# 103 products of zeros in several array forms, issued behind TensorE's warm-up

## The chip, the cores and the metric

The kernel runs on one core of one Trainium2 chip. The metric is the device time of one execution in microseconds (us); the times given are those of undisturbed executions.

## The reference

A block over 2048 rows of width 512. The input is normalized once, and the sum of three terms is returned: the input, an attention over 32 heads of width 16, and a gated MLP whose gate mixes the rows with a 2048 x 2048 matrix.

```
xn = layernorm(x)                                   # x: 1 x 2048 x 512
# attention: 32 heads, head width 16
q, k, v = split(xn @ wqkv)                          # wqkv: 512 x 1536
A = (softmax(q @ k.T * 16**-0.5) @ v) @ wo          # per head; wo: 512 x 512
# gated MLP: inner width 2 x 896
z = gelu(xn @ w_in)                                 # w_in: 512 x 1792
g = w_sp @ layernorm(z[:, 896:]) + b_sp             # w_sp: 2048 x 2048
B = (z[:, :896] * g) @ w_out                        # w_out: 896 x 512
return x + A + B                                    # all in float32
```

## The kernel before

All work of the program is written out ahead of time; each engine runs its own list in order, and a planner in the kernel (`rollout`, `length`) chose TensorE's order for the long phase.

**Front phase.** `load_x` loads the rows in four groups of four tiles of 128 rows. `norm_x` computes mean and variance on VectorE (L391, L392), the factors on ScalarE and VectorE (L394 to L396) and normalizes on ScalarE (L400). `turn_x` transposes the tiles on TensorE (L408) into banks of PSUM; `split` copies each bank as a high part on ScalarE (L78) and subtracts it for a low part on VectorE (L218), which gives `xnT`. Products of the front phase take three multiplications of such parts each (`mm3`, L221 to L223). `v_first` and `v_tile` make the values `v` (L546, L549), `qk_group` the first queries and keys. The weights are split by GpSimd (L1165, L322, L327, L328), partly by VectorE (L322).

**Long phase.** It runs over 16 pairs of heads, four chunks of 512 queries and 16 tiles of keys. TensorE's array is used in several forms there. A *half* is a product of up to 64 rows by 128 columns on the upper or lower half of the rows: the scores (`score`, `st`, L1291), the products from which the maxima are taken (`mx`, L922), and the dense products of the MLP and of the projections (L233). Two halves stand side by side. A *column quad* is four products of 128 rows by 32 columns, side by side on the columns, in plain float32: the product of the weights with the values (`pv`, `o`, L1249). At the end come products of 32 rows (L1109) and quads of another width (L1071).

**Ahead of it all** stands the warm-up: `WARM = 15` products of zeros over the whole array, from the tile `idle` (a piece of the `big` ring, `RING = 25` buffers), which VectorE clears at L1146. They write a bank of PSUM that nobody reads. TensorE's next entry behind them is the first transposition of `turn_x`, L408. The banks `r0` to `r4` are handed out by `rsum`; the first four go to `turn_x`.

A tile of the type `F32R` is multiplied in one pass; the same bytes seen as `F32` (`bitcast`) leave two records per product in the trace.

Of the kernel before, what the change touches and what calls it, by code (L numbers as in the profile page):

```python
# [11 lines left out]
F32 = mybir.dt.float32  # L12
# [7 lines left out]
P = 128  # L20
# [35 lines left out]
def fused_block(ctx, tc, x, wqkv, wo, w_in, w_spT, b_sp, w_out, out):  # L56
    nc = tc.nc
# [5 lines left out]
    ps = ctx.enter_context(tc.tile_pool(name="ps", bufs=1, space=PSUM))  # L63
# [52 lines left out]
    def raw(t):  # L116
        return t.bitcast(F32) if t.dtype == F32R else t
# [3 lines left out]
    def move(dst, src):  # L121
        dma[0] = max(dma[0], clock()) + 0.1 + 4e-6 * math.prod(dst.shape) / FLOW
        nc.sync.dma_start(raw(dst), raw(src))
# [71 lines left out]
    def piece(nm):  # L195
        return big.tile([P, 2, 512], F32R, tag="big", name=nm, bufs=RING)
# [167 lines left out]
    def load_x(g):  # L364
        xt = [at.tile([P, 2, D], F32, tag="pf", name=f"x{g}_{i}", bufs=PF) for i in (0, 2)]
        for i in range(len(xt)):
            k = 2
            t = 4 * g + k * i
            for j in range(k):
                xs[g, k * i + j] = xt[i][:, j, :]  # L370
            if g == 0:
                for j in range(k):
                    move(xt[i][:, j, :], x[(t + j) * P:(t + j + 1) * P, :])
                    yield
            else:
                move(xt[i], x[t * P:(t + k) * P, :].rearrange("(a p) d -> p a d", p=P))
# [758 lines left out]
    def init_rows(a):  # L1135

        for j in range(2):
            row = 64 * j + KS
            for r in range(2):
                nc.gpsimd.dma_start(raw(kst[a])[row + r:row + r + 1, :], cscr[0:1, :])  # L1140

    engines = {mybir.EngineType.PE, mybir.EngineType.Activation, mybir.EngineType.DVE, mybir.EngineType.Pool, mybir.EngineType.SP}
    with tc.manual_schedule(engines=engines):
        nc.scalar.activation(mhalf, epst, AF.Sqrt)
        idle = piece("idle")
# [2 lines left out]
        rest = dpsum("idle", "o")  # L1148
        for _ in range(WARM):
            nc.tensor.matmul(rest, idle[:, 0, 0:P], idle[:, 0, :], start=True, stop=True)  # L1150
        first = load_x(0)
        next(first)
        next(first)
# [488 lines left out]
```

## Time and profile before

| | |
|---|---|
| median of 2 runs | 1789.35 us (1789.29 to 1789.4) |
| span of the profiled execution | 1786.8 us |
| what the median has beside that span | 2.55 us |
| TensorE busy (matmul) | 1775.9 us, 99%, 14419 records |
| TensorE busy (weight load) | 1136.6 us, 64% |
| VectorE busy | 1448.4 us, 81% |
| ScalarE busy | 1267.0 us, 71% |
| GpSimd busy | 782.2 us, 44% |
| mean granted TensorE clock | 0.999 |

The profile is of one execution on the chip. PE is TensorE's multiplication, PEld its weight load, DVE VectorE, ACT ScalarE, POOL GpSimd, SP SyncE. In the timeline a row gives start and length in us, engine, line of the kernel, operation, output and inputs, the form (rows*columns), the shape and a count; in brackets stands the idle time before it and what ended it. A matmul's end is modelled, and records of successive products overlap; therefore distances are best taken from start to start. In a table of stages each engine has its busy time and its number of instructions; PEclk is the clock that TensorE was granted.

### The profile page before, as it was taken

The page shows a single profiled execution, that of the slowest core. Times are in us where ns is not written, and L with a number is a line of the kernel's source. Part 1 is how long each engine was busy: PE and PEld are TensorE (multiplying, and loading weights), DVE is VectorE, ACT ScalarE, POOL GpSimd, SP SyncE. Part 2 cuts the span into 40 slices and gives each one's busy share as a digit, 9 for nine tenths or more (in the row PEclk, how much of TensorE's full clock was granted, in tenths as well). Part 3 has the DMA queues.
Part 4 walks back from the last instruction along what each step waited for, and adds up shares of the span by engine and source line. Part 5 has one row for each costly group of instructions (what it writes and reads, how often), then busy time and mean ns, then how long its engine had stood idle before and what let it go on. Part 6 is the DMA issues. An engine that isn't in the chain of part 4 may idle for free.

```text
span 1786.8 us, 37962 instructions
## 1 busy us (share of the span) xinstructions
PE 1775.9 (99%) x14419; PEld 1136.6 (64%) x14419; DVE 1448.4 (81%) x2604; ACT 1267.0 (71%) x2351; POOL 782.2 (44%) x815
## 2 busy tenths in 40 slices
PE   9999999999999999999999999999999999999998
PEld 7876666666666666656566566666666666666664
DVE  5288888988888888888888888888877888888872
ACT  5338788887777777777777777777776777677765
POOL 4257677777312542257334573224765261004220
PEclk9999999999999999999999999999999999999999
DMA  8552443534645744355446564345666454454534
GB/s 287 200 168 77 133 128 102 171 88 125 199 151 171 234 133 111 115 167 181 135 142 178 171 193 117 105 126 165 197 181 176 145 171 134 147 170 150 155 113 135
DMA packets 218254, 274.63 MB, mean 154 GB/s; under 512 B 35752, under 2 KB 119352, under 8 KB 216632
## 3 DMA queue, kind: packets, MB, share of 16 engines
q1 hardware_dynamic: 215336, 263.47, 48.8%
q0 software_dynamic: 2592, 8.46, 1.2%
q8 instruction: 114, 1.87, 0.5%
q14 instruction: 68, 0.56, 0.1%
q10 hardware_dynamic: 144, 0.26, 0.0%
HBM read 178.55 MB, written 93.58 MB: 152 GB/s over the span
## 4 chain that ended last, share of the span: by engine, by line
PE 97%; DVE 1%; DMA 1%; ACT 1%; POOL 0%; SPq 0%; issue 0%; DVEq 0%; ACTq 0%; POOLq 0%
PE o L1249 26%; PE st L1291 18%; PE sp L233 17%; PE mx L922 13%; PE z2p L233 5%; PE mo L233 4%; PE z1p L233 4%; PE ao L233 2%; PE qk L233 2%; PE duo L233 2%; PE v L221 0%; PE v L222 0%; PE v L223 0%; PE xT L408 0%; PE qk L223 0%; PE qk L221 0%
## 5 line engine op out<-in xcount | busy, mean ns | idle before, releaser
L923 DVE TENSOR_REDUCE mm<-mx 128x1 f32<-128x512 f32 x2048 | 1290.6, 684 | 249.5 <-PE mx L922 216.3
L1294 ACT ACTIVATE pf<-st 128x512 f32<-128x512 f32 x2048 | 1102.6, 601 | 362.3 <-PE mx L922 216.8
L1291 PE MATMUL st<-qst,kst 50*128 50x512 f32 x2048 | 764.4, 410 | 0.9 <-ACT pf L1294 0.7
L922 PE MATMUL mx<-kst,qst 48*128 48x512 f32 x2048 | 752.5, 412 | 0.1
L1291 PEld LDWEIGHTS st<-qst,kst 50*128 50x128 f32 x2048 | 361.1, 185 | 248.6 <-issue 116.3
L233 PE MATMUL sp<-wsp,zs 64*128 64x512 f32 x2688 | 510.1, 393 | 0.0
L1249 PE MATMUL o<-pf,vall 128*32 128x512 f32 x4096 | 492.5, 598 | 0.0
L922 PEld LDWEIGHTS mx<-kst,qst 48*128 48x128 f32 x2048 | 361.7, 185 | 65.2 <-ACT pf L1294 12.4
L233 PEld LDWEIGHTS sp<-wsp,zs 64*128 64x128 f32 x2688 | 365.2, 186 | 30.8
L1249 PEld LDWEIGHTS o<-pf,vall 128*32 128x32 f32 x4096 | 107.0, 109 | 235.5 <-issue 215.9
L233 PE MATMUL mo<-wout,hp 64*128 64x512 f32 x672 | 124.5, 392 | 0.0
L233 PEld LDWEIGHTS mo<-wout,hp 64*128 64x128 f32 x672 | 90.9, 186 | 8.6
L557 POOL TENSOR_TENSOR hhl<-z1i 128x512 f32<-128x512 f32 x28 | 29.2, 1043 | 145.7 <-DMA z1i<-z1scr 145.7
L78 ACT ACTIVATE e<-o 128x512 f32<-128x512 f32 x64 | 38.3, 599 | 69.8 <-PE o L1249 65.6
L879 POOL TENSOR_TENSOR xr<-mox,xr 128x512 f32<-128x512 f32 x8 | 10.3, 1284 | 131.0 <-ACT mox L78 131.0
L563 POOL TENSOR_SCALAR hhl<-hhl 128x512 f32<-128x512 f32 x28 | 17.4, 622 | 105.3 <-ACT hhl L78 105.3
L985 POOL TENSOR_TENSOR ob<-ob 128x512 f32<-128x512 f32 (+1 forms) x16 | 20.6, 1288 | 95.6 <-DMA ob<-rscr 93.4
L823 POOL TENSOR_TENSOR hhl<-hhl,brow 128x512 f32<-128x512 f32 x12 | 15.5, 1290 | 83.4 <-ACT hhl L78 80.7
L233 PE MATMUL ao<-wo,op 64*128 64x512 f32 x288 | 51.8, 392 | 0.0
L604 POOL TENSOR_TENSOR z<-z,z2u 128x896 fp32r<-128x896 f32 x16 | 34.1, 2129 | 27.5 <-ACT z2u L78 27.5
L1057 POOL TENSOR_TENSOR fin<-aox,fin 128x512 f32<-128x512 f32 x8 | 10.3, 1281 | 74.3 <-ACT aox L78 74.3
L233 PEld LDWEIGHTS ao<-wo,op 64*128 64x128 f32 x288 | 36.4, 186 | 4.5
(301 smaller groups left out, 1950.6 us busy)
## 6 DMA issues: line engine op xcount, KB each, us to landing
zs<-z2scr SPq DMA_DIRECT2D x112, 512.0 KB
escr<-e SPq DMA_DIRECT2D x60, 256.0 KB
hscr<-hhl SPq DMA_DIRECT2D x28, 512.0 KB
xscr<-xnT POOLq DMA_DIRECT2D x16, 512.0 KB, 5.2
qscr<-qkhl SPq DMA_DIRECT2D x16, 512.0 KB
kscr<-qkhl SPq DMA_DIRECT2D x16, 512.0 KB
qst<-qscr SPq DMA_DIRECT2D x128, 64.0 KB
hp<-hscr SPq DMA_DIRECT2D x16, 512.0 KB
```

The costliest lines, as they stand in the source:

```text
L78: return nc.scalar.activation(out, in_, func, **kw)
L233: made[half] = lambda: nc.tensor.matmul(acc, prod[0][rows], prod[1][rows], start=start, stop=stop)
L557: gps(0.0022 * n).tensor_mul(u, x, x)
L563: gps(0.0011 * n).tensor_scalar(u, u, a, a, ALU.mult, ALU.add)
L604: gps(2.1).tensor_sub(low, z, u)
L823: gps(1.3).tensor_add(t, t, brow)
L922: nc.tensor.matmul(acc, qst[c][rows, t * P:(t + 1) * P], kst[p % 2][rows, kc * 512:(kc + 1) * 512], start=True, stop=True)
L923: nc.vector.tensor_reduce(mmax[i // 16][:, j, t, kc:kc + 1], acc, AX.X, ALU.max)
L985: gps(1.3).tensor_mul(both[rows, 0, :], both[rows, 0, :], both[rows, 2, :])
L1249: nc.tensor.matmul(acc[cols:cols + VW, a:a + w], vpack(kt - 1 + r, 2 * p + j), pf[:, j * 512 + a:j * 512 + a + w], start=kt == 1 and a == ...
L1291: nc.tensor.matmul(st, kst[p % 2][rows, kt * P:(kt + 1) * P], qst[c][rows, :], start=True, stop=True)
L1294: nc.scalar.activation(full[n][:, j * 512:(j + 1) * 512], st, AF.Exp, scale=0.25)
```

## The change

A function `forms` is added, and called once, behind the warm-up products and ahead of the first load. It issues 103 products of `idle`, all zeros, into four banks that nobody reads. In order:

- ten halves, alternating between the upper 64 rows and the lower 64;
- two column quads over all rows (each four products of 32 columns, in plain float32);
- eight halves;
- four column quads of 64 rows, alternating between the halves of the rows;
- eight halves;
- for each half of the rows: twice a column quad on it and four halves on the other, then six halves alternating;
- five products of 128 rows by 32 columns, all on the first 32 columns;
- four products over the whole array.

```diff
+    def forms(idle):
+        plain = idle.bitcast(F32)
+        banks = [ps.tile([P, 512], F32, tag=f"r{i}", name=f"form{i}", bufs=1) for i in range(4)]
+        def half(h):
+            rows = slice(64 * h, 64 * h + 64)
+            nc.tensor.matmul(banks[h], idle[rows, 0, 0:P], idle[rows, 0, :], start=True, stop=True)
+        def quad(acc, rows):
+            for u in range(4):
+                cols = slice(32 * u, 32 * u + 32)
+                nc.tensor.matmul(acc[cols], plain[rows, 0, cols], plain[rows, 0, :], start=True, stop=True)
+        def both(n):
+            for _ in range(n):
+                half(0)
+                half(1)
+        both(5)
+        for _ in range(2):
+            quad(banks[2], slice(0, P))
+        both(4)
+        for _ in range(2):
+            for h in range(2):
+                quad(banks[2 + h], slice(64 * h, 64 * h + 64))
+        both(4)
+        for h in range(2):
+            for _ in range(2):
+                quad(banks[2 + h], slice(64 * h, 64 * h + 64))
+                for _ in range(4):
+                    half(1 - h)
+            both(3)
+        for _ in range(5):
+            nc.tensor.matmul(banks[2][0:32], idle[:, 0, 0:32], idle[:, 0, :], start=True, stop=True)
+        for _ in range(4):
+            nc.tensor.matmul(banks[3], idle[:, 0, 0:P], idle[:, 0, :], start=True, stop=True)
...
         for _ in range(WARM):
             nc.tensor.matmul(rest, idle[:, 0, 0:P], idle[:, 0, :], start=True, stop=True)
+        forms(idle)
         first = load_x(0)
```

## The prediction

> **What bounds the kernel now.** I read the page first, for its busy shares and for the chain that ended last, then the same span cut into stages, then TensorE's own waits and the timeline around the place of the change.
>
> ```profile
> span 1786.8 us, 37962 instructions
> ...
> PE 1775.9 (99%) x14419; PEld 1136.6 (64%) x14419; DVE 1448.4 (81%) x2604; ACT 1267.0 (71%) x2351; POOL 782.2 (44%) x815
> ...
> PE 97%; DVE 1%; DMA 1%; ACT 1%; POOL 0%; SPq 0%; issue 0%; DVEq 0%; ACTq 0%; POOLq 0%
> ```
>
> TensorE is busy for 99% of the span, and 97% of the chain that ended last lies on it. The next engine, VectorE, has 81%. So whatever delays TensorE delays the end, unless an idle stretch takes the delay up. How much idle time is there, and where?
>
> ```profile
> 6.60:8.06 1.46, 0.31 (x2) 0.14 (x1) 0.95 (x2) 1.41 (x2) 1.46 (x2) 1.00 1.03 386
> 8.06:16.50 8.44, 7.97 (x39) 6.12 (x40) 5.85 (x15) 4.66 (x12) 8.18 (x11) 1.00 1.06 373
> 16.50:130.00 113.50, 112.25 (x693) 90.32 (x694) 60.52 (x116) 43.86 (x78) 42.14 (x54) 1.00 0.58 203
> 130.00:1700.00 1570.00, 1569.74 (x12982) 989.04 (x12980) 1334.85 (x2387) 1161.99 (x2157) 715.66 (x733) 1.00 0.50 150
> ```
>
> In this view of stages column one is the stage in us from the span's start, column two its length, column three TensorE's busy time; the third number from the end is the granted clock. Idle are 1.15 us between the warm-up and 8.06, 0.47 us up to 16.5, 1.25 us up to 130, and 0.26 us in the 1570 us behind that. All the slack between the warm-up and the tail is about 3 us.
>
> The place of the change is the gap behind the fifteen warm-up products:
>
> ```profile
> 1.55 5.05 PE L1150 MATMUL idle<-idle 128*128 128x512 f32 x15 [1.55 <-DVE idle L1146]
> 7.45 0.30 PE L408 MATMUL xT<-ident,x 128*128 128x128 f32 x1 [0.84 <-ACT x L400]
> 8.06 0.98 PE L408 MATMUL xT<-ident,x 128*128 128x128 f32 x7 [0.31 <-ACT x L400]
> ```
>
> The warm-up ends at 6.60. The first transposition of real data comes at 7.45, the second at 8.06, and each had waited for ScalarE's normalized `x`. From 8.06 on nothing that TensorE does was waiting for the warm-up. A delay shorter than about 1.5 us would be free here; the rest is passed on.
>
> **The change, part by part.** It removes and moves nothing. It adds 103 products of zeros to TensorE's queue behind the warm-up and ahead of the first transposition: 54 halves (64 rows by 128 columns), 40 products in 10 column quads (32 columns each, plain f32; two quads over all rows, eight over one half), and 9 over all rows (five of 32 columns, four of 128). No DMA is issued, and no other engine's queue gets an instruction. No new product needs anything but `idle`, which the warm-up already uses, and the four banks have no tenant yet, so none waits for another engine. Behind them on TensorE's queue waits everything: the transpositions, then ScalarE and VectorE (`xnT`), the v products, the stores. The `idle` buffer is given back later, but 24 other pieces are taken before its slot of the 25 comes round again, which the code reaches only with the last row group of the first phase.
>
> So the cost is the length of this chain. I take it in units from the steady part, where such forms run all the time:
>
> ```profile
> 500.54 0.39 PE L1291 MATMUL st<-qst,kst 50*128 50x512 f32 x1
> 500.54 0.39 PE L922 MATMUL mx<-kst,qst 48*128 48x512 f32 x1
> ...
> 501.24 0.39 PE L1291 MATMUL st<-qst,kst 50*128 50x512 f32 x1
> ...
> 503.57 0.39 PE L1291 MATMUL st<-qst,kst 50*128 50x512 f32 x1
> 503.88 1.92 PE L1249 MATMUL o<-pf,vall 128*32 128x512 f32 x16
> 505.74 0.50 PE L1291 MATMUL st<-qst,kst 50*128 50x512 f32 x1
> ...
> 506.08 0.40 PE L1291 MATMUL st<-qst,kst 50*128 50x512 f32 x1
> ```
>
> Two halves start together, and the next pair but two starts 0.70 us later: 0.233 us per **pair of halves**. L1249 is the column quad in f32; each of its products leaves two records, so 16 records are two quads, and from the first quad to the next half pass 505.74 - 503.88 = 1.86 us.
>
> ```profile
> 504.77 1.04 PE L1249 MATMUL o<-pf,vall 128*32 128x512 f32 x8
> ```
>
> In a narrower window the second quad (its eight records, the later ones of those 16) starts at 504.77, so the first took 0.89, and the second with the way back to a half 0.97. One quad alone, with the way back, I set at 1.00. A **change of form** costs beyond that: 0.32 from the last half's start to the first quad's (503.57 to 503.88) where a pair is 0.233, and 0.34 from the first pair behind a quad to the second (505.74 to 506.08). Products over all rows follow each other at 0.228:
>
> ```profile
> 30.04 0.39 PE L221 MATMUL qk<-xnT,wqk 128*128 128x512 f32 x1
> ...
> 30.95 0.39 PE L222 MATMUL qk<-xnT,wqk 128*128 128x512 f32 x1
> ```
>
> (0.91 us for four.) The sum goes by starts, from the last warm-up product's, 6.60 - 0.39 = 6.21:
>
> 1. Five pairs: 0.32 + 0.34 + 3 x 0.233 = 1.36, to 7.57.
> 2. Two quads over all rows, then four pairs: 0.32 + 1.86 + 0.34 + 2 x 0.233 = 2.99, to 10.56.
> 3. Two quads on each half, then four pairs. No row shows quads of 64 rows. If the halves run side by side, each two cost what one costs over all rows: 2.99 again, to 13.55. If in turn, 2 x 0.86 = 1.72 more. It cannot be less than one quad's time for each two. Four quarters side by side (L1249) and two halves side by side (L1291 with L922) are the nearest rows; I take side by side.
> 4. The mixed part, for each half: twice a quad on it and four halves on the other, then three pairs. If the forms take turns: 2 x (0.32 + 1.00 + 0.34 + 2 x 0.233) = 4.25, and three more halves on the busier side, 0.70: 4.95; for both 9.90, to 23.45. If they run side by side, a cycle is the longer of 0.86 and 4 x 0.233 = 0.93: 0.32 + 0.93 + 0.97 + 0.34 + 0.23 = 2.79, for both 5.58, which is 4.3 less.
> 5. Five products of 32 columns on one quarter, so one behind the other: 0.32 + 0.34 + 3 x 0.23 = 1.35 (no row shows this form alone; a pass of L1249's quad, half of 0.86, would make it 0.43 each and 1.0 more, and 0.2 less than summed is left if the first needs no 0.34), to 24.80. Four over all rows: 0.32 + 0.34 + 2 x 0.23 = 1.12, to 25.92; the first transposition 0.23 later, 26.15.
>
> Does part 4 take turns? All switches seen wait until the old form has ended, also this one, of another pair of forms:
>
> ```profile
> 1736.16 0.39 PE L1291 MATMUL st<-qst,kst 50*128 50x512 f32 x1
> 1736.48 1.33 PE L1109 MATMUL al<-sel,on 32*128 32x512 f32 x8
> ```
>
> Again 0.32 us from a half to a 32-row form. But in each case the new form wants rows that the old one holds, so the trace leaves open what happens on separate halves. I take turns, since no two forms stand side by side anywhere in it. The Trainium skill, "TensorEngine Tiling (Array Packing)", section Key Properties, has two rules that pull apart here: a change of tiling mode, not only of tile, drains TensorE; and separate tiles can load and multiply in parallel. By the first this part costs the 9.90 above, by the second 5.58; no run here shows it yet.
>
> **Where the delay lands.** The transpositions are ready long before, so the second follows the first at 0.11 (seven from 8.06 in 0.98 with the last one's tail). It starts at 26.26 where it was at 8.06: 18.2 us late. Little of this can be won back, since VectorE's queue is in order: the next statistics stand behind `xnT`, which waits for the transpositions. What is late next is that chain, unchanged. GpSimd's casts however are done by then, and no longer run beside VectorE:
>
> ```profile
> 6.48 0.69 DVE L322 TENSOR_TENSOR wv<-wv0r,wv 128x512 fp32r<-128x512 f32 x1
> ...
> 11.79 0.92 DVE L322 TENSOR_TENSOR kst<-wv2r,kst 128x512 fp32r<-128x512 f32 x1
> ...
> 12.82 0.37 DVE L396 SCALAR_TENSOR_TENSOR rs<-mv,rs 128x2 f32<-128x2 f32 x1
> ...
> 14.80 0.98 PE L408 MATMUL xT<-ident,x 128*128 128x128 f32 x7 [0.38 <-ACT x L400]
> ...
> 20.54 0.16 DVE L396 SCALAR_TENSOR_TENSOR rs<-mv,rs 128x2 f32<-128x2 f32 x1
> ```
>
> L396 took 0.37 with GpSimd at work and 0.16 later; L322 took 0.92, and 0.69 at 6.48. That is 0.4 us of the chain that ends in the wait at 14.80; I take 0.4 off (none to 0.5). Beyond 130 us 0.26 us of idle time can give back nothing. Delay: 17.8 us. The profiled execution is 1786.8 us, and the median 1789.35 has 2.55 us around that; both shift alike: 1789.35 + 17.8 = **1807.2 us**, 1.0% slower, which is within the 2% (35.8 us) that a measurement here can tell from no change.
>
> **The rivals.**
>
> - *The mixed part runs side by side.* For it: halves and quarters do so among themselves. Against it: each change of form in the trace costs its 0.32. It saves 4.3: 13.5 us, **1802.8**.
> - *Quads of 64 rows run in turn too.* For it: no row shows eight at once. 1.72 more: 19.5 us, **1808.9**.
> - *The clock falls under the thin forms* (the other side). The warm-up began at half the pace at which it ended:
>
> ```profile
> 1.55 1.65 PE L1150 MATMUL idle<-idle 128*128 128x512 f32 x3 [1.55 <-DVE idle L1146]
> 5.51 0.86 PE L1150 MATMUL idle<-idle 128*128 128x512 f32 x3
> ```
>
>   At the start three records span 1.65 us, at the end 0.86. Should the pace fall back with the first halves, all from 6.53 to 26.15 would double, 19.6 more: 37.4 us, **1826.8**, slower by 2.1%. It passes the 2% if at least 18.0 of the 19.6 us run so. Against it: the steady part is made of halves and quads, holds its 0.233 us per pair at 501, and has a granted clock of 1.00.
> - *The change does nothing*, since no one reads its banks and the products could be dropped: **1789.4**. Against it: nobody reads the warm-up's bank either, and its 15 records stand there.
>
> **How the numbers follow.** Turns in the mixed part, the rest as summed: 0.52, with 1805 to 1809 as its own range (1 us for part 5, 0.4 for the chain, and about 0.1 for each of the changes of form). Side by side 0.27; quads in turn 0.13; clock 0.03; nothing 0.01; the rest, two of these at once, 0.04. The range must hold the first three: 1802.8 less 1.3 to 1808.9 plus 1.1, **1801.5 to 1810**. Faster by over 2%: 0.01, slower by over 2%: 0.03, within: 0.96.
>
> **What would show it.** In the changed profile's timeline the first transposition should stand near 26.2 and the second 0.11 behind it; TensorE should be busy throughout from 1.55; the four pairs of part 2 should start 1.9 us behind their first quad. In part 4 the records decide: halves that start within 0.1 us of a quad's are side by side, halves 1.0 us behind it take turns. Behind 30 us each event should stand 17.8 us later than before. The forecast is wrong if the quads of 64 rows or the mixed part cost other than summed, if pairs follow each other at more than 0.233 between 7 and 26, or if more than 1 us comes back between 30 and 130.

## The result, and the profile after

The changed kernel takes 1807.22 us (two runs, 1806.23 and 1808.2) against 1789.35 us: ratio 1.010 (95% interval 1.0071 to 1.0129), 17.9 us more. The forecast was 1807.2, so the sum came out; the terms did not all do so, and the profiled execution, the slower of the two runs, is 19.5 us longer than that of before (1806.3 against 1786.8 us).

The page of the changed kernel, for the totals that the prediction began with:

```profile
span 1806.3 us, 38248 instructions
...
PE 1796.4 (99%) x14562; PEld 1149.4 (64%) x14562; DVE 1448.8 (80%) x2604; ACT 1267.0 (70%) x2351; POOL 780.6 (43%) x815
...
PE 96%; DMA 2%; DVE 1%; ACT 0%; POOL 0%; SPq 0%; issue 0%; DVEq 0%; POOLq 0%
```

TensorE has 143 records more (54 halves, 80 for the forty f32 products, 9 others) and 20.5 us more busy time; the other engines do what they did. The timeline of TensorE at the place of the change (L1189 is the warm-up now, L1150 the halves, L1155 the quads, L1177 and L1179 the products over all rows):

```profile
1.55 6.43 PE L1189 MATMUL idle<-idle 128*128 128x512 f32 x15 [1.55 <-DVE idle L1185]
7.92 1.42 PE L1150 MATMUL form<-idle 64*128 64x512 f32 x10
9.27 1.92 PE L1155 MATMUL form<-idle 128*32 128x512 f32 x16
11.12 1.20 PE L1150 MATMUL form<-idle 64*128 64x512 f32 x8
12.25 1.95 PE L1155 MATMUL form<-idle 64*32 64x512 f32 x32
14.13 1.20 PE L1150 MATMUL form<-idle 64*128 64x512 f32 x8
15.25 1.06 PE L1155 MATMUL form<-idle 64*32 64x512 f32 x8
16.25 1.18 PE L1150 MATMUL form<-idle 64*128 64x512 f32 x4
17.36 1.06 PE L1155 MATMUL form<-idle 64*32 64x512 f32 x8
18.35 1.89 PE L1150 MATMUL form<-idle 64*128 64x512 f32 x10
20.17 1.06 PE L1155 MATMUL form<-idle 64*32 64x512 f32 x8
...
25.09 1.33 PE L1177 MATMUL form<-idle 128*32 128x512 f32 x5
26.26 1.09 PE L1179 MATMUL form<-idle 128*128 128x512 f32 x4
27.19 1.04 PE L408 MATMUL xT<-ident,x 128*128 128x128 f32 x8
```

Three things are to be seen. No row has idle time in front of it: from 1.55 until the first transpositions TensorE never waits. The 32 records of the 64-row quads take 1.95 us, as long as the 16 of two quads over all rows (1.92): eight tiles do stand side by side. And in the mixed part the halves start 1.00 us behind their quad (16.25 against 15.25) and the next quad 1.11 us behind them: quad and halves take turns, though they hold different rows.

The fourth thing is in the first row. The warm-up's fifteen products span 6.43 us, where they spanned 5.05 before. The same products of the same zeros took 1.38 us longer in this execution, because the pace changed from 0.43 to 0.23 us per product only at about 7.4 us instead of 4.4. The granted clock that the view gives for these stretches is 1.00 before the change of pace as well as behind it, so that column does not show the slow start, and what sets the moment of the change stays open. (The expectations below call it the opening, or the rise, of the clock.)

What is left of the shift further down can be followed from two marks: the first query product (the first of L221 on `qk`) and the last column quad. From the traces, starts in us:

| profile of | last warm-up product | second transposition | from there to the first query product | from that to the last column quad's records |
|---|---|---|---|---|
| before | 6.21 | 8.06 | 14.05 | 1754.05 |
| changed | 7.60 | 27.30 | 13.53 | 1754.85 |

So the second transposition is 19.24 us late, 0.52 come back in the front phase, and 0.8 are lost again in the long one.

### The profile page after: what moved, and what is told of

Same layout as the page of the kernel before. It is cut to its first block, busy times and chain, and to the rows that moved or that the text cites. A ratio compares the mean times of both kernels' runs of the same rounds, so it can differ in the third digit from the quotient of the medians.

```text
span 1806.3 us, 38248 instructions
## 1 busy us (share of the span) xinstructions
PE 1796.4 (99%) x14562; PEld 1149.4 (64%) x14562; DVE 1448.8 (80%) x2604; ACT 1267.0 (70%) x2351; POOL 780.6 (43%) x815
## 4 chain that ended last, share of the span: by engine, by line
PE 96%; DMA 2%; DVE 1%; ACT 0%; POOL 0%; SPq 0%; issue 0%; DVEq 0%; POOLq 0%
PE o L1289 26%; PE st L1331 17%; PE sp L233 17%; PE mx L922 13%; PE z2p L233 5%; PE mo L233 4%; PE z1p L233 3%; PE qk L233 2%; PE ao L233 2%; PE duo L233 2%; PE v L221 1%; PE v L222 1%; PE v L223 1%; PE form L1150 1%; DMA rscr<-os 0%; PE form L1155 0%
```

## The experiments

Twelve runs were made, two of them repeats: of the kernel before, and of one of the experiments. The times beside them are of the kernel before on the same chip, which differs by up to 1.5 us from chip to chip (1788.66 to 1790.17). The runs whose argument lies in the timeline alone have one time each, which differs with the start of the warm-up too.

**What makes the mixed part take turns?** Quad and halves differ in two ways, in the tile form and in the type of number. One kernel takes the first difference away, another the second.

```diff
-                quad(banks[2 + h], slice(64 * h, 64 * h + 64))
+                rows = slice(64 * h, 64 * h + 64)
+                nc.tensor.matmul(banks[2 + h], plain[rows, 0, 0:P], plain[rows, 0, :], start=True, stop=True)
```

> The mixed part with one plain f32 product of 64 rows by 128 columns in place of each column quad, beside the same four halves. Theory (the tile form makes the turns): both now have the form of 64 by 128, so they stand side by side in spite of their two types. A cycle is the longer of 0.86 and 4 x 0.233 = 0.93 us, no change of form is paid, and from the last half of the part before to the last half of the mixed part I expect about 2 x (2 x 0.93 + 0.70) = 5.1 us where the changed kernel has 9.84; the whole is 4.7 us faster than it. Rival (the two types of number make the turns): each cycle stays a sum, 0.86 + 0.93 and a change of about 0.3, and the part stays above 9 us.

Its timeline in the mixed part (L1173 is the f32 product of 64 by 128, L1150 the halves):

```profile
14.05 0.59 PE L1173 MATMUL form<-idle 64*128 64x512 f32 x1
14.05 0.62 PE L1150 MATMUL form<-idle 64*128 64x512 f32 x2
14.48 0.59 PE L1173 MATMUL form<-idle 64*128 64x512 f32 x1
14.52 0.62 PE L1150 MATMUL form<-idle 64*128 64x512 f32 x2
14.91 0.59 PE L1173 MATMUL form<-idle 64*128 64x512 f32 x1
```

Both sides start at 14.05, with no change of form, and the f32 product's passes go on every 0.43 us beside the halves. The part takes 4.94 us from last half to last half, where I had said 5.1, and 9.84 in the changed kernel; the kernel takes 1800.92 us with 1790.17 beside it. The type is not what makes the turns. The counterpart:

```diff
-                for _ in range(4):
-                    half(1 - h)
+                rows = slice(64 * (1 - h), 64 * (1 - h) + 64)
+                nc.tensor.matmul(banks[1 - h], plain[rows, 0, 0:P], plain[rows, 0, :], start=True, stop=True)
```

> The mixed part with one plain f32 product of 64 rows by 128 columns on the other half in place of the four halves, so that both sides are f32 and only the tile form differs. Theory (tile form): they take turns; the product starts about 1.0 us behind the quad's start, the next quad about 1.0 us behind the product's, some 2.0 us per cycle. Rival (type): they start together, within 0.1 us, and a cycle is 0.86 us.

```profile
14.26 1.06 PE L1155 MATMUL form<-idle 64*32 64x512 f32 x8
15.25 1.12 PE L1174 MATMUL form<-idle 64*128 64x512 f32 x2
16.31 1.06 PE L1155 MATMUL form<-idle 64*32 64x512 f32 x8
```

Both f32, and still the product starts 0.99 us behind the quad and the next quad 1.06 behind the product: 2.05 us per cycle (1806.54 us for the kernel). The tile form decides, on separate rows too. The Trainium skill's rule in "TensorEngine Tiling (Array Packing)", Key Properties, that a change of tiling mode drains TensorE, is borne out: 0.99 us on rows that the quad did not hold.

**Is a change of form free at the end of the list?** I had charged 0.32 and 0.34 us between the five products of 32 columns and the four of 128; the profile has 0.231 and 0.233 there. In one kernel the five were made plain f32.

```diff
-            nc.tensor.matmul(banks[2][0:32], idle[:, 0, 0:32], idle[:, 0, :], start=True, stop=True)
+            nc.tensor.matmul(banks[2][0:32], plain[:, 0, 0:32], plain[:, 0, :], start=True, stop=True)
```

> The five products of 128 rows by 32 columns in plain f32 instead of the one-pass type, all on the first quarter. In the changed kernel the four whole-array products followed these five at 0.231 us with no cost for a change of form. Theory (the one-pass type runs a 32-column product in the form of the whole array, so no form changed there): now the form does change; the five take 5 x 0.86 = 4.3 us, and from the last second pass to the first whole-array product I expect 0.43 + 0.09 = 0.52 us, and 0.34 to the second. Rival (quarters to whole array is a free change): 0.43 to the first and 0.23 to the second.

```profile
24.76 4.48 PE L1177 MATMUL form<-idle 128*32 128x512 f32 x10
29.17 1.19 PE L1179 MATMUL form<-idle 128*128 128x512 f32 x4
30.20 1.03 PE L408 MATMUL xT<-ident,x 128*128 128x128 f32 x8
```

The ten passes start every 0.43 us, the last at 28.65; the first whole-array product follows at 29.17, 0.52 later, and the second 0.34 behind that. So the change is paid for f32, and not for the one-pass type. The kernel takes 1810.72 us with 1790.17 beside it, as the ten f32 passes take longer than the five products did. The likely reading, that the one-pass type with 32 columns runs in the form of the whole array, fits both; it is inferred, not seen.

**Do the forms matter to what comes behind, and is all of it passed on?** Two kernels.

```diff
-        both(5)
...
+        for _ in range(85):
+            nc.tensor.matmul(banks[3], idle[:, 0, 0:P], idle[:, 0, :], start=True, stop=True)
```

> 85 products over the whole array in place of the 103, of about the same length: 85 x 0.2285 = 19.4 us. Theory (only the time that TensorE's queue is held matters, not the forms): first transposition about 19.65 us behind the last warm-up start, as with the forms (19.59), time 1807 us within the scatter of the clock's opening (1 us either way). Rival (the forms themselves upset something later, banks or queue): a time away from the changed kernel's by more than 2 us.

Measured: 1806.75 us (four runs) against 1788.66, ratio 1.0103 (1.0089 to 1.0117); the first transposition stands at 25.87, 19.50 behind the last warm-up product at 6.37. 18.1 us for 85 plain products, 17.9 for the 103 in their forms, on another chip: a difference that can't be told from none, so the forms upset nothing further down.

```diff
-        both(5)
...
+        for _ in range(2):
+            both(5)
...
```

> The whole list of forms issued twice. Theory (all of it is passed on to the end): another 0.32 + 0.34 + ... , the list's own 19.4 us, so 1826.6 us, 37 us over the kernel before, 2.1% slower. Rival (something behind takes part of the delay up, so that the second one costs less): less than 18 us over the changed kernel.

Measured: 1826.01 us against 1788.66, ratio 1.0208 (1.0194 to 1.0222), so 37.4 us for two lists. The second list costs 19.5 us, the whole of its length on TensorE's queue: nothing behind takes any of it up. The first cost 17.9, since the gap in front of the rows took a part and the front phase gave some back.

**What is the warm-up worth now?**

```diff
-WARM = 15
+WARM = 0
```

> The forms without the fifteen warm-up products. Theory (warm-up products now lie on the path, and thin forms raise the clock as well as whole ones): the list starts at 1.55 at half pace and the clock rises after 3 to 6 us; the list needs 19.6 us and half of the cold stretch more, so the first transposition comes at 22.6 to 24.1, 15 x 0.23 = 3.4 us earlier than with the warm-up: 1803.8 us. Rival (products of half the rows or a quarter of the columns do not raise the clock): the list runs at half pace until its whole-array end, the first transposition comes near 40, and the time is near 1820 us.

Measured: 1803.78 us against 1788.66, ratio 1.0085 (1.0071 to 1.0098); the first transposition is at 22.35, just under the 22.6 to 24.1 expected. In the timeline the list begins slowly and is at full pace from its second part's end on:

```profile
1.56 2.50 PE L1150 MATMUL form<-idle 64*128 64x512 f32 x10 [1.56 <-DVE idle L1185]
3.99 2.39 PE L1155 MATMUL form<-idle 128*32 128x512 f32 x16
6.31 1.20 PE L1150 MATMUL form<-idle 64*128 64x512 f32 x8
7.44 1.95 PE L1155 MATMUL form<-idle 64*32 64x512 f32 x32
```

The ten halves span 2.50 us instead of 1.42, the two quads 2.39 instead of 1.92, the rest is as before. So thin forms bring the full pace as whole ones do (here 3.4 us after the first product), and the warm-up, once something stands behind it, costs about 3 us (1806.75 with it, for the list of whole products on the same chip).

**Is a short list free?** Only the first five pairs were kept.

```diff
         both(5)
-        for _ in range(2):
-            quad(banks[2], slice(0, P))
...
```

> Only the first five pairs of halves remain of the added products. Theory (a gap in front of the first real work takes up what is short, and the rest is passed on): the five pairs end about 1.6 us behind the last warm-up product's start; where the clock opens early (last warm-up start 6.2) they are over before the second transposition at 8.06 and cost nothing, where it opens late (7.6) they cost about 1.2 us. So 1789.3 to 1790.6, and the runs scatter more than those of the kernel before (0.1 us). Rival (any product added in front costs its time): 1.4 us more in every run, 1790.7, with no more scatter than before.

Measured: 1790.21 us (eleven runs, 1789.91 to 1791.39) against 1788.66 (fifteen, 1787.95 to 1789.41), ratio 1.001 (1.0001 to 1.0019). This is 1.5 us, more than the 0 to 1.2 that my theory allowed, and the scatter is the same in both kernels, not larger. By its number the rival wins; the profile shows another way to it:

```profile
7.26 1.43 PE L1150 MATMUL form<-idle 64*128 64x512 f32 x10
8.84 1.06 PE L408 MATMUL xT<-ident,x 128*128 128x128 f32 x8
...
12.71 1.75 POOL L328 TENSOR_TENSOR wqk<-wqk_0r,wqk 128x512 fp32r<-128x512 f32 x1
12.76 0.29 ACT L394 ACTIVATE rs<-mv,epst 128x2 f32<-128x2 f32 x1 [2.27 <-DVE mv L392]
13.43 1.05 DVE L396 SCALAR_TENSOR_TENSOR rs<-mv,rs 128x2 f32<-128x2 f32 x1
14.52 1.52 ACT L400 ACTIVATE x<-x,rs 128x512 f32<-128x512 f32 x2 [1.46 <-DVE rs L396]
```

The last pair starts at 8.30, and the transposition 0.54 behind it, not 0.32: the transposition waits for a semaphore that TensorE's own last halves raise, as one of them wrote bank `r0`, which it writes next; the long list had left `r0` well before. (That the change of form alone would be 0.32 here too is taken from the other changes.) The second transposition is at 8.97, 0.91 late. Then L396, two elements per row, takes 1.05 us; it ends at 14.48, and GpSimd's L328 at 14.46. The small delay has pushed it beside a longer GpSimd instruction. This accounts for the front phase of this profile alone; how the 1.5 us of the median divide is not shown. A second profile of the same kernel was to show whether this repeats:

> The five pairs behind the fifteen once more, for a second profile. Theory: the first transposition comes 0.54 us behind the last pair (0.32 for the change of form and 0.22 for a wait of TensorE on its own last product in the bank that it writes next), whenever the clock opens; L396 takes 0.4 to 1.1 us and ends together with the GpSimd instruction beside it. Rival: without the wait, 0.32 us, and L396 at 0.16.

Its last warm-up product starts at 7.65, the last pair at 9.00, the transposition at 9.54: 0.54 again. L396 takes 0.38 beside a GpSimd cast, and ends at 14.61 where the cast ends at 14.59. The one run took 1790.77 us with 1789.65 beside it: with the second transposition at 9.68 it lost about as much, though L396 was short. And the same five pairs behind a shorter warm-up:

```diff
-WARM = 15
+WARM = 8
```

> Five pairs of halves behind eight warm-up products instead of fifteen, so that TensorE is free by 7.2 us at the latest, whenever the clock opens. Theory (what ends ahead of the normalized rows is free; the five pairs cost 1.5 us behind fifteen because they ended later than these, then waited 0.22 us for their own bank, and moved VectorE's L396 into a longer GpSimd instruction): second transposition at 8.0 to 8.1 and the time of the kernel before, within 0.5 us. Rival (any added product costs its own time at the end): about 1.4 us more than before, as with fifteen, or 0.2 us less for the seven left out.

Measured: 1789.47 us (eleven runs) against 1789.65 (fifteen), ratio 0.9999 (0.999 to 1.0008). In the profile the pairs are over at 7.51 and the second transposition is at 7.80, though the pace rose late in that run:

```profile
1.56 3.78 PE L1172 MATMUL idle<-idle 128*128 128x512 f32 x8 [1.56 <-DVE idle L1168]
5.27 2.25 PE L1150 MATMUL form<-idle 64*128 64x512 f32 x10
7.66 1.06 PE L408 MATMUL xT<-ident,x 128*128 128x128 f32 x8
```

So the five pairs cost nothing where they end in time, and the rival's 1.4 us falls. Its other figure, 0.2 less for the seven products left out, is not told from none by these times (0.18 less); against it stands the repeat of the kernel before, further down, whose warm-up ended 1.3 us later at no cost. In front of the list of this change there was simply less room than the one profile showed. (The first query product came at 22.86 in this profile, 0.75 later than in that of before, behind two subtractions L322 of 1.1 us each; over the runs this does not show.)

**Who held VectorE?** GpSimd was kept at work until after the delayed chain:

```diff
         nc.gpsimd.memset(vall[:, NT * H * (DH + 1):], 0.0)
+        nc.gpsimd.memset(brow, 0.0)
+        for _ in range(15):
+            nc.gpsimd.tensor_sub(brow, brow, brow)
```

> The changed kernel with one memset and fifteen subtractions of 128 by 512 on GpSimd behind its last memset, about 1.3 us each, so that it is at work from 12 to about 35 us, when VectorE makes the second pair of normalized tiles. Theory (VectorE was slower beside GpSimd, and the change won 0.47 us back because GpSimd had finished): L322 goes back from 0.67 to about 0.9 us, L396 from 0.16 to about 0.37, and the transposition of the third tile starts about 5.9 to 6.0 us behind the second one's group as in the kernel before, 0.4 us or so later than in the changed kernel. Rival (it was the DMA traffic, or ScalarE): the rows stay as in the changed kernel.

In the changed kernel, where GpSimd had finished at 16:

```profile
30.97 0.67 DVE L322 TENSOR_TENSOR kst<-wv2r,kst 128x512 fp32r<-128x512 f32 x1
31.08 0.29 ACT L394 ACTIVATE rs<-mv,epst 128x2 f32<-128x2 f32 x1 [2.27 <-DVE mv L392]
31.75 0.16 DVE L396 SCALAR_TENSOR_TENSOR rs<-mv,rs 128x2 f32<-128x2 f32 x1
```

and with GpSimd at work:

```profile
29.91 0.76 DVE L322 TENSOR_TENSOR kst<-wv2r,kst 128x512 fp32r<-128x512 f32 x1
30.03 0.30 ACT L394 ACTIVATE rs<-mv,epst 128x2 f32<-128x2 f32 x1 [2.27 <-DVE mv L392]
30.21 1.62 POOL L328 TENSOR_TENSOR wqk<-wqk_0r,wqk 128x512 fp32r<-128x512 f32 x1
30.78 1.07 DVE L396 SCALAR_TENSOR_TENSOR rs<-mv,rs 128x2 f32<-128x2 f32 x1
```

L396 takes 1.07 instead of 0.16 and ends at 31.85, GpSimd's L328 at 31.83. The kernel took 1806.43 us in its one run, with 1790.17 beside it; the 0.4 us expected on top of the changed kernel's time can't be seen in single runs. From the second transposition to the first query product it is 14.51 us; in all seven kernels with a list of 60 products or more and GpSimd done, the changed one among them, it is 13.53 or 13.54. So the half microsecond that came back is VectorE's freedom from GpSimd. I had expected L322 to grow to about 0.9, which it did not (0.76), and L396 to 0.37, which it passed. The Trainium skill, "SBUF — State Buffer", section Who interferes with whom, has the rule: a VectorE instruction with two inputs from SBUF and a GpSimd instruction that reads SBUF exclude each other; the common ends, 31.85 and 31.83 here, agree. Which of the two is held is not so clear: in the profile with eight warm-up products L322 started at 12.35, 0.58 us ahead of a GpSimd cast, and still took 1.11 us instead of 0.67.

The reverse was tried on the kernel before, as a version that might beat both:

```diff
-        w0 = [end(l) for l in w0]
         run(norm)
         v_first(wv, lambda: turn_x(0, 2, 4))
+        w0 = [end(l) for l in w0]
```

> The kernel before with GpSimd's two pairs of weight splits (L327, L328) moved behind the first value tiles, so that none runs beside VectorE's L322 and L396 at 11.8 to 13.2. Theory (those two were held by GpSimd): L322 near 0.67, L396 near 0.16, the third tile's transposition 5.7 us behind the second one's instead of 6.04, and the first query product 0.4 us earlier, at about 21.7, unless the weights are late for it, which GpSimd finishes at about 20.5 for the first half and 22.4 for the second. Rival (DMA traffic held them): L322 and L396 stay at 0.92 and 0.37, and the rows behind stay where they were.

```profile
11.91 0.68 DVE L322 TENSOR_TENSOR kst<-wv2r,kst 128x512 fp32r<-128x512 f32 x1
12.03 0.30 ACT L394 ACTIVATE rs<-mv,epst 128x2 f32<-128x2 f32 x1 [2.67 <-DVE mv L392]
12.69 0.16 DVE L396 SCALAR_TENSOR_TENSOR rs<-mv,rs 128x2 f32<-128x2 f32 x1
```

The two rows are as short as expected, and from ScalarE's L394 to the next seven transpositions it is 2.43 us instead of 2.89. But the front phase as a whole did not gain: 14.00 us from the second transposition to the first query product against 14.05, where 0.4 less was expected. The chain began later: an earlier subtraction, L322 on `wv1r`, ended at 9.05 instead of 8.75, behind a GpSimd cast that had waited 1.11 us for its DMA in this execution. One run gave 1789.58 us, with 1789.65 for the kernel before: no gain that can be told from none.

**Was the rest of the shift the change's?** The kernel before, once more:

> The kernel before once more, for a second profile. Theory: the last warm-up product starts anywhere from 6.2 to 7.6, as the clock opens, without moving the second transposition at 8.0 to 8.1; and the long phase by itself moves its end by up to 0.7 us against the first profile, in one or two places where a DMA comes late. Rival (the long phase repeats to 0.1 us, and what the changed kernel lost there came from the change): the distance between transposition and last column quad is the same in both.

```profile
1.56 6.37 PE L1150 MATMUL idle<-idle 128*128 128x512 f32 x15 [1.56 <-DVE idle L1146]
7.77 1.04 PE L408 MATMUL xT<-ident,x 128*128 128x128 f32 x8
```

Its last warm-up product started at 7.54, 1.3 us later than in the first profile, and the second transposition at 7.88, 0.2 earlier: there the late change of pace cost nothing, in a profile of the same span (1786.8 us). From the first query product to the last column quad it took 1754.34 us, after 1754.05 in the first profile. Over the fourteen profiles of this study, with the same work in that stretch, it ranges from 1753.24 to 1755.61. One of the places is a DMA that comes late now and then; in the changed kernel's profile:

```profile
619.66 0.47 PE L1331 MATMUL st<-qst,kst 50*128 50x512 f32 x1 [0.46 <-DMA qst<-mscr]
```

This wait is about half of the 0.8 us that the changed kernel lost there; the rest is not placed. All of it is within what the long phase does by itself.

## Why the prediction was right, point by point

| step | predicted, us | measured, us |
|---|---|---|
| last warm-up product starts | 6.21 | 7.60 |
| part 1, to the first quad | 1.68 | 1.67 |
| part 2, from first quad to first 64-row quad | 2.99 | 2.98 |
| part 3, side by side | 2.99 | 3.00 |
| part 4, in turns | 9.90 | 9.84 |
| part 5, to the first transposition | 2.38 | 2.10 |
| second transposition behind the first | 0.11 | 0.11 |
| won back in the front phase | 0.4 | 0.52 |
| lost or won in the long phase | 0 | 0.8 lost, in this execution |

- *What bounds.* Right: TensorE's queue, and all behind it is passed on. Two lists cost 37.4 us, one 17.9.
- *The units.* 0.233 per pair, 0.86 per quad, 0.32 and 0.34 for a change of form, taken from 500 us into the run, held at 8 us to a few hundredths.
- *The two open questions of the change* came out as taken: 64-row quads side by side, the mixed part in turns. The argument for turns was weak, that no two forms stood side by side in the trace, since there each new form also wanted the old one's rows. The two experiments on the mixed part settled it.
- *Part 5* was over by 0.28: I charged a change of form behind the five products of 32 columns that is not paid in their type (0.20 of it), and 0.34 to the second of the five, which came after 0.25.
- *The start of the list* was the step that failed. I took 6.21 for the last warm-up product as if it were a property of the kernel. It was 6.2 to 7.65 in the twelve profiles with fifteen warm-up products, and 7.60 in the changed kernel's. Before, that was hidden, as the transpositions came at 7.8 to 8.1 in any case; behind the list it counts.
- *The free room of 1.5 us* was overstated for the same reason, and because the first transposition waits 0.22 us for TensorE's own last product when that is in its bank: five pairs, 1.36 us, cost 1.5.
- *What was won back* has its cause right, GpSimd. But L322's 0.69 at 6.48 was no case without GpSimd: a cast ran beside it from 6.53 and took 1.11 us, where others took 0.61. That L322 takes about this long undisturbed (0.67 in the changed kernel) was luck in the choice of the row.
- The profile's 19.5 us are 17.8, with 1.39 for the warm-up, less 0.35 for the list and 0.1 for the half microsecond won back, with 0.8 in the long phase. That the median of two runs hits the forecast to 0.02 us is luck: the two runs lie 2 us apart, and the largest of these terms are about a microsecond each.
- *The rivals.* Side by side (1802.8) falls. How well its saving was sized is not shown: with equal forms the part takes 4.94, but the 5.58 said had changes of form in it, which no run shows side by side. 64-row quads in turn falls (1.95 us for 32 records). Half pace under thin forms falls: from the last warm-up product to the first transposition it is 19.59 us, where half pace would need twice that. The granted clock of 1.00 that I held against it was no evidence, since the view gives 1.00 for the slow start of the warm-up too. That the products are dropped falls: the 143 records are there.

## What to carry to other kernels

Price a list of products by start-to-start times of the same forms elsewhere in the trace, and charge about 0.1 us for each change from halves to column tiles (0.32 where a pair takes 0.233) and 0.2 for the way back (0.52 where a pass takes 0.43, then 0.34 where a product takes 0.233); grouping work by form, not by type of number, is what lets halves of the array run side by side. Before calling a gap in front of real work free, look at what ends it and at what starts it in more than one execution: a warm-up's end moved by 1.4 us here. A chain that shifts against another engine's list can win or lose half a microsecond by what it then stands beside.

## What was not expected of the hardware

- The pace of the array nearly doubled (from 0.43 to 0.23 us per product) 2.9 to 6.0 us after the first product, in different executions of like kernels (for instance at 4.4 us and 7.3 us from the start in the two profiles of the kernel before, whose products begin at 1.55).
- A VectorE instruction of two elements per row, L396, took from 0.16 to 1.07 us by what GpSimd did beside it. GpSimd's L328 took 1.62 and 1.75 us instead of 1.28 at the same places; there it had started 0.3 us behind the start of VectorE's L322, or less, and it ended 1.1 to 1.2 us behind L322's end.
- The one-pass products of 32 columns pass to whole-array products with no cost for the change (0.231 us), plain f32 ones with 0.52 and 0.34.
